# Joining the weighted sums of one attention tile to the scores of the next in a fused attention and MLP kernel, and loading the last batch tile by tile

## The chip, the cores and the metric

The kernel runs on one core of one Trainium2 chip. The metric is the device time of one execution in microseconds (us). The kernel before was run six times: the median is 226.07 us, the lowest 225.56, the highest 226.84. One further number belongs to one of these executions, which took 225.72 us: the hardware profiler recorded it, and everything that is read from a profile below comes from it.

## The reference, cut to what matters

Attention with 4 batches, 8 heads, 768 positions and 64 values a head. A position sees the 128 positions up to itself (the window) and the first four positions of the sequence (the sinks). The heads are laid side by side, and a normalised two-layer MLP with 512 inputs and 2048 hidden values is added to them.

```
scores = q @ k.T / 8
keep   = (pos_k < 4) | (0 <= pos_q - pos_k < 128)
a = softmax(where(keep, scores, -1e9))
x = concat_heads(a @ v)                      # 4 x 768 x 512
xn = (x - mean(x)) / sqrt(var(x) + 1e-6) * g
out = x + relu(xn @ w1) @ w2                 # w1 512x2048, w2 2048x512
```

## The kernel before, in words

The 4 x 768 rows are 24 **tiles** of 128 rows, six to a batch (`RB`); tile t has r = t % 6. The engines are TensorE (PE), VectorE (DVE), ScalarE (ACT) and GpSimd (POOL); SyncE (SP) issues DMAs, and POOL issues the casting loads.

**Attention of a tile** is two TensorE steps with exponentials between them.

- `scores(t)` (lines 548 to 610) multiplies the keys of block r with the queries of blocks r and r + 1, because a key block is seen by its own queries and by those of the next block. A head has 64 values, so the two heads of a pair lie in the two halves of the array's rows: one matmul on rows 0 to 63, one on rows 64 to 127 (L574), with the results in two PSUM banks. Eight matmuls of 256 columns make a tile (128 columns in the last tile of a batch). ACT takes the exponential of each half of four heads (L585, 128x1024), and DVE (L595) or POOL (L597, L600) clears what lies outside the window.
- `values(t)` (lines 620 to 727) sums the values with these weights: 16 matmuls of 65 columns (64 values and a column of ones that gives the divisor), eight with this tile's weights (L641) and eight with those of the tile before (L644). From r = 2 on the sinks lie outside the window, so two more matmuls of 260 columns (L634, one for four heads) add them first; their weights `es` and values `vs` are made once a batch by `sinks`. `es` and `vs` are block structured: heads 0 to 3 fill rows 0 to 63, heads 4 to 7 rows 64 to 127, yet each of the two matmuls runs over all 128 rows. DVE then divides (`recip`, L666 and L668), takes mean and variance (`stat`, L674 and L677) and centres and scales (`cen`, L682). From tile 10 on a DMA transpose on SP's queue (L711) lays the result out for the MLP as `xnt`.

**The MLP** works on groups of 2, 2, 2, 4, 4, 4, 4 and 2 tiles. `up` (L745) makes 128 hidden values for a group of four tiles in four matmuls of 512 columns, and ACT or DVE takes the maximum with zero. `down` (L785) makes a quarter of a tile's output in four matmuls of 512 columns; after the fourth quarter DVE adds x (L798), and SP stores it (L803).

**PSUM** is held by hand. Slots 0 and 2 are the two `wide` tiles of two banks each (kind "pw"); slots 4 to 7 are the four `single` banks (kind "pm"). Scores take both wide tiles (one in the last tile of a batch), `values` takes one wide tile, `up` and `down` take one single bank at a time.

**The order of the work** is a planner's. Every step is an `Op` with a cost for each engine, the steps that it depends on, buffers and a key. `Plan.emit` (lines 57 to 160) goes through a model of the engines, and among the steps that could start first on the engine it takes the one with the lowest key. What it emits is a fixed order for each engine's queue; engines wait by semaphores, in order. `attention(t, key)` (lines 811 to 816) gives the scores of tile t, then `values(t - 1)` as a separate step with nearly the same key, and after the last tile of a batch that tile's own `values`. Batch 0 has an order of its own (lines 849 to 872).

**Loads.** Batches 2 and 3 take q and k in twelve blocks each (`load_qk`, L398, POOL's queue), which DMA transposes on SP's queue turn (`prep`, L481); v comes in six blocks (`load_v`, L407). At most seven loads are under way. The twelve loads of batch 3 stand one behind the other as soon as batch 2 has been turned, and so do its twelve transposes.

Of the kernel before, what the change touches and what calls it, by code (L numbers as in the profile page):

```python
# [8 lines left out]
FP32 = mybir.dt.float32  # L9
# [22 lines left out]
class Plan:  # L32
# [18 lines left out]
    def op(self, engs, fn, deps=(), key=0.0, alloc=(), uses=(), lat=0.0):  # L51
        o = Op(engs, fn, deps, key, alloc, uses)
        o.lat = lat
        self.ops.append(o)
        return o
# [108 lines left out]
def kernel(  # L164
# [28 lines left out]


    GROUPS = [2, 2, 2, 4, 4, 4, 4, 2]
    NB0 = 3
    NG = len(GROUPS)
    FIRST = [sum(GROUPS[:g]) for g in range(NG)]
# [33 lines left out]
    def room_for(buf):  # L232
        return wide[buf.slot // 2] if buf.pool == "pw" else single[buf.slot - 4]
# [252 lines left out]
    def ready(b, hps, klo, khi, qlo, qhi):  # L486

        ends = ((qlo, qhi), (klo, khi))
        if b in CHUNKS:
            w = S // CHUNKS[b]  # L490
            return [prepped[(b, c, hp, x)] for c in range(CHUNKS[b]) for hp in hps for x in range(2)
                    if c * w < ends[x][1] and (c + 1) * w > ends[x][0]]
        return [prepped[(b, r, x)] for x in range(2) for r in range(RB)
                if 128 * r < ends[x][1] and 128 * (r + 1) > ends[x][0]]
# [50 lines left out]

    ebuf = {}

    def scores(t, halves, key):

        b, r = divmod(t, RB)  # L550
        kb = kqb[b]
        last = r == RB - 1
        n = 128 if last else 256

        parts = [halves] if last else [(half,) for half in halves]
        pbs, ebs = [Buf("pw", 0) for _ in parts], [Buf("e", 8) for _ in parts]
        for eb, part in zip(ebs, parts):
            for half in part:
                ebuf[(t, half)] = eb

        added = t < NEG_TILES

        def mm(_):
            for pb, eb, part in zip(pbs, ebs, parts):
                eb.t = epool.tile([128, 2, 512 // n, n], BF16, name="e")
                pb.t = room_for(pb).rearrange("p a (i c) -> p a i c", c=n)
                if added:
                    neg = (neg1 if r else neg0)[:, 0:n].unsqueeze(1).to_broadcast([128, 2, n])
                    for h2 in range(2):
                        nc.tensor.matmul(pb.t[:, h2], lhsT=ident, rhs=neg,  # L570
                                         start=True, stop=False, skip_group_check=True)
                for i, hp in enumerate([2 * half + i for half in part for i in range(2)]):
                    for h2 in range(2):
                        nc.tensor.matmul(pb.t[:, h2, i],  # L574
                                         lhsT=kb.t[64 * h2:64 * (h2 + 1), 1, hp, 128 * r:128 * (r + 1)],
                                         rhs=kb.t[64 * h2:64 * (h2 + 1), 0, hp, 128 * r:128 * r + n],
                                         start=not added, stop=True, skip_group_check=True)

        cost = 0.2 + 0.23 * n / 256 * len(halves) + (0.43 * len(halves) if added else 0.0)
        hps = [2 * half + i for half in halves for i in range(2)]  # L580
        o0 = op({"PE": cost}, mm, ready(b, hps, 128 * r, 128 * (r + 1), 128 * r, 128 * r + n) + [neg_done, edone.get((t - 1, 1)) if last else None], key, pbs + ebs, [kb])

        for pb, eb, part in zip(pbs, ebs, parts):
            def ex(_, pb=pb, eb=eb):
                nc.scalar.activation(eb.t, pb.t, AF.Exp, scale=scale)  # L585

            def first(_, eb=eb):
                ev = eb.t.rearrange("p a i c -> p (a i) c")
                nc.vector.tensor_tensor(ev, ev, mask0.unsqueeze(1).to_broadcast([128, 4, 256]), op=ALU.mult)

            def window(e, eb=eb):
                ev = eb.t.rearrange("p a i c -> p (a i) c")
                m = 1024 // n
                if e == "DVE":
                    nc.vector.tensor_tensor(ev, ev, mask1[:, 0:n].unsqueeze(1).to_broadcast([128, m, n]), op=ALU.mult)  # L595
                    return
                nc.gpsimd.affine_select(out=ev[:, :, 0:128], in_=ev[:, :, 0:128], compare_op=ALU.is_ge,  # L597
                                        fill=0.0, base=0, pattern=[[0, m], [1, 128]], channel_multiplier=-1)
                if n > 128:
                    nc.gpsimd.affine_select(out=ev[:, :, 128:256], in_=ev[:, :, 128:256], compare_op=ALU.is_gt,  # L600
                                            fill=0.0, base=0, pattern=[[0, m], [-1, 128]], channel_multiplier=1)

            o = op({"ACT": 1.02}, ex, [o0], key, (), [eb, pb])
            if not added:
                if r == 0:
                    o = op({"DVE": 0.69}, first, [o, masks_done], key, (), [eb])
                else:
                    o = op({"POOL": 1.28, "DVE": 0.69}, window, [o, masks_done], key, (), [eb])
            for half in part:
                edone[(t, half)] = o  # L610
# [6 lines left out]
    xb, xnb, xtb, mvb, rsb, turned = {}, {}, {}, {}, {}, {}  # L617
    aggr = {}

    def values(t, key):  # L620
        b, r = divmod(t, RB)
        g, ti = where[t]
        vn, vs = vn_buf[b % 2], vs_buf[b % 2]
        pb = Buf("pw", 0)
        xb[t] = Buf("x", 14)
        xnb[t] = Buf("xn", 6)

        def mm(_):
            po = pb.t = room_for(pb)
            pv = po[:, :, 0:4 * (D + 1)].rearrange("p a (h d) -> p a h d", d=D + 1)  # L630
            for half in range(2):
                fresh = True
                if r >= 2:
                    nc.tensor.matmul(po[:, half, 0:4 * (D + 1)], lhsT=esb[b].t[:, 128 * (r - 2):128 * (r - 1)],  # L634
                                     rhs=vs[:, 4 * half:4 * half + 4, :].rearrange("p h d -> p (h d)"),
                                     start=True, stop=False, skip_group_check=True)
                    fresh = False
                for hh in range(4):
                    i, h2 = divmod(hh, 2)
                    h = 4 * half + hh  # L640
                    nc.tensor.matmul(pv[:, half, hh, :], lhsT=weights_of(t, half, i, h2, 0), rhs=vn[:, r, h, 0:D + 1],  # L641
                                     start=fresh and hh == 0, stop=(r == 0), skip_group_check=True)
                    if r > 0:
                        nc.tensor.matmul(pv[:, half, hh, :], lhsT=weights_of(t - 1, half, i, h2, 128),  # L644
                                         rhs=vn[:, r - 1, h, 0:D + 1], start=False, stop=True, skip_group_check=True)

        deps = [edone[(t, half)] for half in range(2)] + [vcast[(b, r)], ones_done]
        uses = [ebuf[(t, half)] for half in range(2)]
# [5 lines left out]
        if r >= 2:  # L654
            deps += [sunk[b], vs_done[b]]
            uses += [esb[b]]
            cost += 0.22
        o = op({"PE": cost}, mm, deps, key, [pb], uses)
        vread[(b, r)] = o

        rc = {}

        def recip(_):
            pv = pb.t[:, :, 0:4 * (D + 1)].rearrange("p a (h d) -> p a h d", d=D + 1)
            rc[0] = small.tile([128, 2, 4], FP32, name="rc")
            nc.vector.reciprocal(rc[0], pv[:, :, :, D])  # L666
            xb[t].t = xpool.tile([128, H, D], BF16, name="xt")
            nc.vector.tensor_tensor(xb[t].t.rearrange("p (a h) d -> p a h d", a=2), pv[:, :, :, 0:D],  # L668
                                    rc[0].unsqueeze(3).to_broadcast([128, 2, 4, D]), op=ALU.mult)

# [11 lines left out]
            nc.vector.scalar_tensor_tensor(xnb[t].t, in0=xf, scalar=mvb[g][:, ti, 0:1], in1=gb,  # L682
                                           op0=ALU.subtract, op1=ALU.mult)

        o = op({"DVE": 0.92}, recip, [o], key, [xb[t]], [pb])
        o = op({"DVE": 0.9}, stat, [o], key, (), [xb[t]])
        aggr[t] = o
        o = op({"DVE": 0.75}, cen, [o, gb_done], key, [xnb[t]], [xb[t]])
# [120 lines left out]


    def attention(t, key):
        scores(t, (0, 1), key)
        if t % RB:
            values(t - 1, key - 0.5)
        if t % RB == RB - 1:
            values(t, key + 1.0)


# [28 lines left out]
    for b in range(B):  # L847
# [25 lines left out]
        if b == 1:  # L873
            for hp in range(HP):
                prep_runs(1, 0, hp, k0 - 12 + 3 * hp)
        else:
            for r in range(RB):
                for x in range(2):
                    load_qk(b, x, r, k0 - 60 + r, [prepped.get((b - 1, RB - 1, 1))])
            for r in range(RB):  # L880
                load_v(b, r, k0 - 50 + r, [prepped[(b, RB - 1, 1)]])
        for r in range(RB):
            attention(RB * b + r, akey(RB * b + r))
            if r == 1:
                sinks(b, akey(RB * b + 2) - 1)
# [54 lines left out]
```

The softmax here doesn't subtract the row's maximum and nothing guards it: scores larger than these inputs give would overflow.

## Time and profile before

| what | value | where from |
|---|---|---|
| median of six runs | 226.07 us | the times |
| profiled execution | 225.72 us | the times |
| its span | 224.0 us | head of the page |
| PE busy | 217.3 us, 97% | part 1 |
| DVE busy, ACT busy, POOL busy | 114.8 us (51%), 111.7 us (50%), 81.2 us (36%) | part 1 |
| granted TensorE clock | full in all slices | part 2 |
| L745 and L785, share of the chain that ended last | 37% and 34% | part 4 |
| L634, L641, L644 (values) busy | 8.7, 15.8, 14.2 us | groups by form |
| L574 (scores) busy | 14.5 us | part 5 |

The span is what the profiler saw from the first to the last instruction; the time has 1.7 us more around it. Matmul records overlap, since a matmul's record reaches to the end of its passage through the array: durations of one matmul (380 ns for 512 columns) are longer than the step from its start to the next start. Steps between starts, in the timeline, are what the engine's time is made of.

### The profile page before, as it was taken

The page shows a single profiled execution, that of the slowest core. Times are in us where ns is not written, and L with a number is a line of the kernel's source. Part 1 is how long each engine was busy: PE and PEld are TensorE (multiplying, and loading weights), DVE is VectorE, ACT ScalarE, POOL GpSimd, SP SyncE. Part 2 cuts the span into 40 slices and gives each one's busy share as a digit, 9 for nine tenths or more (in the row PEclk, how much of TensorE's full clock was granted, in tenths as well). Part 3 has the DMA queues.
Part 4 walks back from the last instruction along what each step waited for, and adds up shares of the span by engine and source line. Part 5 has one row for each costly group of instructions (what it writes and reads, how often), then busy time and mean ns, then how long its engine had stood idle before and what let it go on. Part 6 is the DMA issues. An engine that isn't in the chain of part 4 may idle for free.

```text
span 224.0 us, 4431 instructions
## 1 busy us (share of the span) xinstructions
PE 217.3 (97%) x1805; PEld 122.8 (55%) x1826; DVE 114.8 (51%) x216; ACT 111.7 (50%) x159; POOL 81.2 (36%) x111
## 2 busy tenths in 40 slices
PE   7999999999999999999999999999999999999994
PEld 7465878884546455455544444544454554444852
DVE  5566976054969789589474467470026750021011
ACT  3699775687252576860227762147603156400620
POOL 8985876259420799350823000220006020000000
PEclk9999999999999999999999999999999999999999
DMA  7999999999999799999999111330012130012102
GB/s 172 158 191 197 191 208 204 204 159 155 138 128 258 144 156 132 154 130 182 79 162 233 25 23 48 97 93 0 0 45 77 47 97 0 0 47 94 50 0 94
DMA packets 84774, 25.59 MB, mean 114 GB/s; under 512 B 74385, under 2 KB 81809, under 8 KB 84754
## 3 DMA queue, kind: packets, MB, share of 16 engines
q0 software_dynamic: 59392, 13.24, 66.4%
q1 hardware_dynamic: 24818, 11.67, 26.6%
q10 hardware_dynamic: 544, 0.39, 0.5%
q8 instruction: 14, 0.23, 0.4%
q14 instruction: 6, 0.05, 0.1%
HBM read 27.27 MB, written 6.29 MB: 150 GB/s over the span
## 4 chain that ended last, share of the span: by engine, by line
PE 89%; DVE 6%; DMA 2%; issue 1%; ACT 1%; DVEq 0%
PE single L785 37%; PE single L745 34%; PE wide L574 5%; PE wide L641 2%; PE wide L644 2%; DVE st L674 2%; DVE xt L668 2%; DVE xn L682 2%; DMA xnt<-in_q_dram 2%; PE wide L634 1%; PE wide L457 1%; PE wide L570 1%; PE single L721 1%; PE single L236 1%; PE single L457 1%
## 5 line engine op out<-in xcount | busy, mean ns | idle before, releaser
L745 PE MATMUL single<-xnt,w1s 128*128 128x256 bf16 (+1 forms) x503 | 87.1, 325 | 0.6 <-issue 0.2
L745 PEld LDWEIGHTS <-w1s 128*128 128x128 bf16 x512 | 48.4, 98 | 32.8 <-issue 2.4
L585 ACT ACTIVATE e<-wide 128x1024 bf16<-128x1024 f32 x44 | 43.6, 1022 | 43.3 <-PE wide L574 40.7
L785 PE MATMUL single<-w2s,h1t 128*128 128x512 bf16 x249 | 57.6, 379 | 0.4
L798 DVE SCALAR_TENSOR_TENSOR ot<-single,rs,xt 128x512 f32<-128x512 f32 (+2 forms) x25 | 18.2, 729 | 61.6 <-PE single L785 45.1
L754 ACT ACTIVATE h1t<-single 128x512 bf16<-128x512 f32 x60 | 35.8, 597 | 21.1 <-PE single L745 21.1
L785 PEld LDWEIGHTS <-h1t 128*128 128x128 bf16 x256 | 24.0, 98 | 28.2 <-issue 1.1
L785 PE MATMUL single<-w2s,h1n 128*128 128x512 bf16 (+2 forms) x139 | 29.6, 355 | 0.3
L754 ACT ACTIVATE h1n<-single 128x512 bf16<-128x512 f32 x30 | 17.9, 597 | 22.2 <-PE single L745 22.0
L597 POOL TENSOR_SCALAR_AFFINE_SELECT e<-e 128x512 bf16<-128x512 bf16 (+1 forms) x10 | 7.0, 697 | 45.0 <-ACT e L585 45.0
L407 POOL DMA_DIRECT2D vn<-in_v_dram x24 | 21.7, 922 | 2.0 <-DMA qkn<-in_q_dram 1.0
L694 POOL TENSOR_SCALAR ve<-mv 128x2 f32<-128x2 f32 (+1 forms) x8 | 4.6, 574 | 46.5 <-DVE mv L677 46.3
L595 DVE TENSOR_TENSOR e<-e,mask 128x1024 bf16<-128x1024 bf16 x22 | 15.9, 722 | 8.7 <-ACT e L585 8.5
L785 PEld LDWEIGHTS <-h1n 128*128 128x128 bf16 x144 | 12.6, 98 | 12.3 <-issue 1.3
L682 DVE SCALAR_TENSOR_TENSOR xn<-xt,mv,gb 128x512 bf16<-128x512 bf16 x24 | 18.3, 768 | 0.7
L674 DVE BATCH_NORM_STATS2 st<-xt 128x6 f32<-128x512 bf16 x24 | 16.7, 695 | 0.8
L668 DVE TENSOR_TENSOR xt<-wide,rc 128x512 bf16<-128x512 f32 x24 | 16.6, 691 | 0.8
L641 PE MATMUL wide<-vn,e 128*128 128x65 bf16 x192 | 15.8, 193 | 0.0
L641 PEld LDWEIGHTS <-e 128*128 128x128 bf16 x192 | 13.7, 97 | 2.6 <-issue 0.2
L574 PE MATMUL wide<-qkt 64*128 64x256 bf16 (+1 forms) x192 | 14.5, 263 | 0.0
L644 PE MATMUL wide<-vn,e 128*128 128x65 bf16 x160 | 14.2, 193 | 0.0
L398 POOL DMA_DIRECT2D qkn<-in_q_dram x12 | 11.3, 938 | 3.6 <-DMA qkn<-in_k_dram 3.1
(66 smaller groups left out, 161.1 us busy)
## 6 DMA issues: line engine op xcount, KB each, us to landing
out_dram<-ot SPq DMA_DIRECT2D x23, 256.0 KB, 2.2
vn<-in_v_dram POOLq DMA_DIRECT2D x24, 128.0 KB, 8.0
w1s<-in_moe_w_ch_dram POOLq DMA_DIRECT2D x4, 512.0 KB, 11.2
w2s<-in_moe_w_ch_dram POOLq DMA_DIRECT2D x4, 512.0 KB, 15.0
qkn<-in_q_dram POOLq DMA_DIRECT2D x12, 128.0 KB, 7.5
qkn<-in_k_dram POOLq DMA_DIRECT2D x12, 128.0 KB, 7.1
qkn<-in_q_dram POOLq DMA_DIRECT2D x1, 768.0 KB, 16.2
qkn<-in_k_dram POOLq DMA_DIRECT2D x1, 768.0 KB, 19.3
```

The costliest lines, as they stand in the source:

```text
L407: nc.gpsimd.dma_start(vn_buf[b % 2][:, r, :, 0:D], v[b, :, 128 * r:128 * (r + 1), :].rearrange("h p d -> p h d"))
L574: nc.tensor.matmul(pb.t[:, h2, i], lhsT=kb.t[64 * h2:64 * (h2 + 1), 1, hp, 128 * r:128 * (r + 1)], rhs=kb.t[64 * h2:64 * (h2 + 1), 0, hp, ...
L585: nc.scalar.activation(eb.t, pb.t, AF.Exp, scale=scale)
L641: nc.tensor.matmul(pv[:, half, hh, :], lhsT=weights_of(t, half, i, h2, 0), rhs=vn[:, r, h, 0:D + 1], start=fresh and hh == 0, stop=(r == 0 ...
L644: nc.tensor.matmul(pv[:, half, hh, :], lhsT=weights_of(t - 1, half, i, h2, 128), rhs=vn[:, r - 1, h, 0:D + 1], start=False, stop=True, ski ...
L668: nc.vector.tensor_tensor(xb[t].t.rearrange("p (a h) d -> p a h d", a=2), pv[:, :, :, 0:D], rc[0].unsqueeze(3).to_broadcast([128, 2, 4, D] ...
L674: nc.vector.bn_stats(st, xf)
L682: nc.vector.scalar_tensor_tensor(xnb[t].t, in0=xf, scalar=mvb[g][:, ti, 0:1], in1=gb, op0=ALU.subtract, op1=ALU.mult)
L745: nc.tensor.matmul(pb.t[:, n * i:n * (i + 1)], lhsT=w1s[:, j, 128 * (h0 + i):128 * (h0 + i + 1)], rhs=xtb[g].t[:, j, 0:n], start=(j == 0), ...
L754: nc.scalar.activation(hb.t, pb.t, AF.Relu)
L785: nc.tensor.matmul(pb.t[:, 0:n], lhsT=hidden(g, ht, ti), rhs=w2s[:, ht, c0:c1], start=(ht == 0), stop=(ht == NH1 - 1))
L798: nc.vector.scalar_tensor_tensor(ob.t[:, 0:n], in0=pb.t[:, 0:n], scalar=rsb[g][:, ti:ti + 1], in1=xb[t].t.rearrange("p h d -> p (h d)")[:, ...
```

## The change

`values(t - 1)` is no longer a step of its own where it can be joined: `values(..., joined=True)` returns a `Lead` that `scores(t)` runs first, in one planner step, with the dependencies, buffers and costs of both. This holds for t = 11 to 23, so the joined sums are those of tiles 10 to 22; the last tile of batch 1 and of batch 2 is now joined to the first scores of the next batch. Tiles 6 to 9 (`ALONE`), batch 0 and tile 23 keep separate steps.

A joined sum lies in two single banks and not in one wide tile, and DVE divides it in two halves with two instructions each. Its sink matmuls come behind the others and run on 64 rows each, half 0 on rows 0 to 63 and half 1 on rows 64 to 127, with an accumulator bank each.

The q, k and v blocks of batch 3 are asked for one at a time, each with the key of a tile of batch 2 and, from the second on, behind the masks of the tile before (`seen`).

```diff
+    ALONE = (6, 7, 8, 9)
...
-    def scores(t, halves, key):
+    def scores(t, halves, key, lead=None):
...
         def mm(_):
+            if lead:
+                lead.fn(None)
...
+        if lead:
+            o0 = op({"PE": cost + lead.cost}, mm, deps + lead.deps, key, lead.alloc + pbs + ebs, [kb] + lead.uses)
+            lead.rest(o0)
+        else:
+            o0 = op({"PE": cost}, mm, deps, key, pbs + ebs, [kb])
...
-    def values(t, key):
+    def values(t, key, joined=False):
...
-        pb = Buf("pw", 0)
+        banks = [Buf("pm", 0), Buf("pm", 0)] if joined else [Buf("pw", 0)]
...
+        def sink(half, fresh):
+            rows = slice(64 * half, 64 * (half + 1)) if joined else slice(0, 128)
+            nc.tensor.matmul(sums[half], lhsT=esb[b].t[rows, 128 * (r - 2):128 * (r - 1)],
+                             rhs=vs[rows, 4 * half:4 * half + 4, :].rearrange("p h d -> p (h d)"),
+                             start=fresh, stop=not fresh, skip_group_check=True)
...
             for half in range(2):
                 fresh = True
-                if r >= 2:
+                if r >= 2 and not joined:
+                    sink(half, True)
                     fresh = False
...
+            if r >= 2 and joined:
+                for half in range(2):
+                    sink(half, False)
...
-            cost += 0.22
-        o = op({"PE": cost}, mm, deps, key, [pb], uses)
+            cost += 0.12 if joined else 0.22
+        if joined:
+            lead = Lead()
+            lead.fn, lead.deps, lead.alloc, lead.uses, lead.cost = mm, deps, banks, uses, cost
+            lead.rest = lambda o: normalise(t, key, o, banks, sums)
+            return lead
+        normalise(t, key, op({"PE": cost}, mm, deps, key, banks, uses), banks, sums)
...
+            if len(banks) == 2:
+                for half in range(2):
+                    pv = sums[half].rearrange("p (h d) -> p h d", d=D + 1)
+                    rc[half] = small.tile([128, 4], FP32, name=f"rc{half}")
+                    nc.vector.reciprocal(rc[half], pv[:, :, D])
+                    nc.vector.tensor_tensor(xb[t].t[:, 4 * half:4 * half + 4], pv[:, :, 0:D],
+                                            rc[half].unsqueeze(2).to_broadcast([128, 4, D]), op=ALU.mult)
+                return
...
-        o = op({"DVE": 0.92}, recip, [o], key, [xb[t]], [pb])
+        o = op({"DVE": 0.92 if len(banks) == 1 else 1.22}, recip, [o], key, [xb[t]], banks)
...
     def attention(t, key):
-        scores(t, (0, 1), key)
-        if t % RB:
+        alone = t - 1 in ALONE
+        scores(t, (0, 1), key, None if alone or t == RB else values(t - 1, key, True))
+        if alone:
             values(t - 1, key - 0.5)
-        if t % RB == RB - 1:
+        if t == NT - 1:
             values(t, key + 1.0)
...
-            for r in range(RB):
+            for r in range(RB if b == 2 else 0):
                 for x in range(2):
-                    load_qk(b, x, r, k0 - 60 + r, [prepped.get((b - 1, RB - 1, 1))])
+                    load_qk(b, x, r, k0 - 60 + r)
-            for r in range(RB):
+            for r in range(RB if b == 2 else 0):
                 load_v(b, r, k0 - 50 + r, [prepped[(b, RB - 1, 1)]])
         for r in range(RB):
+            if b == B - 2:
+                t = RB * (b + 1) + r
+                seen = [edone[(RB * b + r - 1, 0)]] if r else []
+                for x in range(2):
+                    load_qk(b + 1, x, r, akey(t) - 45, seen + [prepped[(b, RB - 1, 1)]])
+                load_v(b + 1, r, akey(t) - 40, seen)
             attention(RB * b + r, akey(RB * b + r))
```

More of the change, by code (lines that the diff above doesn't have):

```diff
@@ L580, in scores @@
         hps = [2 * half + i for half in halves for i in range(2)]
-        o0 = op({"PE": cost}, mm, ready(b, hps, 128 * r, 128 * (r + 1), 128 * r, 128 * r + n) + [neg_done, edone.get((t - 1, 1)) if last else None], key, pbs + ebs, [kb])
+        deps = ready(b, hps, 128 * r, 128 * (r + 1), 128 * r, 128 * r + n) + [neg_done, edone.get((t - 1, 1)) if last else None]
+        if lead:
[3 more added lines that the diff above has]
+            o0 = op({"PE": cost}, mm, deps, key, pbs + ebs, [kb])
         for pb, eb, part in zip(pbs, ebs, parts):
@@ L618 @@
     aggr = {}
-    def values(t, key):
+    class Lead:
+        pass
+    def values(t, key, joined=False):
         b, r = divmod(t, RB)
@@ L623, in values @@
         vn, vs = vn_buf[b % 2], vs_buf[b % 2]
-        pb = Buf("pw", 0)
+        banks = [Buf("pm", 0), Buf("pm", 0)] if joined else [Buf("pw", 0)]
+        sums = []
         xb[t] = Buf("x", 14)
         xnb[t] = Buf("xn", 6)
+        def sink(half, fresh):
[3 more added lines that the diff above has]
+                             start=fresh, stop=not fresh, skip_group_check=True)
         def mm(_):
-            po = pb.t = room_for(pb)
-            pv = po[:, :, 0:4 * (D + 1)].rearrange("p a (h d) -> p a h d", d=D + 1)
+            po = [room_for(i) for i in banks]
+            po = po if joined else [po[0][:, i] for i in range(2)]
+            sums[:] = [i[:, 0:4 * (D + 1)] for i in po]
             for half in range(2):
                 fresh = True
-                if r >= 2:
-                    nc.tensor.matmul(po[:, half, 0:4 * (D + 1)], lhsT=esb[b].t[:, 128 * (r - 2):128 * (r - 1)],
-                                     rhs=vs[:, 4 * half:4 * half + 4, :].rearrange("p h d -> p (h d)"),
-                                     start=True, stop=False, skip_group_check=True)
+                if r >= 2 and not joined:
+                    sink(half, True)
                     fresh = False
+                pv = sums[half].rearrange("p (h d) -> p h d", d=D + 1)
                 for hh in range(4):
@@ L640, in mm @@
                     h = 4 * half + hh
-                    nc.tensor.matmul(pv[:, half, hh, :], lhsT=weights_of(t, half, i, h2, 0), rhs=vn[:, r, h, 0:D + 1],
+                    nc.tensor.matmul(pv[:, hh, :], lhsT=weights_of(t, half, i, h2, 0), rhs=vn[:, r, h, 0:D + 1],
                                      start=fresh and hh == 0, stop=(r == 0), skip_group_check=True)
                     if r > 0:
-                        nc.tensor.matmul(pv[:, half, hh, :], lhsT=weights_of(t - 1, half, i, h2, 128),
-                                         rhs=vn[:, r - 1, h, 0:D + 1], start=False, stop=True, skip_group_check=True)
+                        nc.tensor.matmul(pv[:, hh, :], lhsT=weights_of(t - 1, half, i, h2, 128),
+                                         rhs=vn[:, r - 1, h, 0:D + 1], start=False, stop=not (joined and r >= 2),
+                                         skip_group_check=True)
+            if r >= 2 and joined:
+                for half in range(2):
+                    sink(half, False)
         deps = [edone[(t, half)] for half in range(2)] + [vcast[(b, r)], ones_done]
@@ L656, in values, with normalise @@
             uses += [esb[b]]
-            cost += 0.22
-        o = op({"PE": cost}, mm, deps, key, [pb], uses)
+            cost += 0.12 if joined else 0.22
[5 more added lines that the diff above has]
+        normalise(t, key, op({"PE": cost}, mm, deps, key, banks, uses), banks, sums)
+    def normalise(t, key, o, banks, sums):
+        b, r = divmod(t, RB)
+        g, ti = where[t]
         vread[(b, r)] = o
@@ L663, in recip @@
         def recip(_):
-            pv = pb.t[:, :, 0:4 * (D + 1)].rearrange("p a (h d) -> p a h d", d=D + 1)
+            xb[t].t = xpool.tile([128, H, D], BF16, name="xt")
+            if len(banks) == 2:
+                for half in range(2):
+                    pv = sums[half].rearrange("p (h d) -> p h d", d=D + 1)
+                    rc[half] = small.tile([128, 4], FP32, name=f"rc{half}")
[3 more added lines that the diff above has]
+                return
+            pv = room_for(banks[0])[:, :, 0:4 * (D + 1)].rearrange("p a (h d) -> p a h d", d=D + 1)
             rc[0] = small.tile([128, 2, 4], FP32, name="rc")
             nc.vector.reciprocal(rc[0], pv[:, :, :, D])
-            xb[t].t = xpool.tile([128, H, D], BF16, name="xt")
             nc.vector.tensor_tensor(xb[t].t.rearrange("p (a h) d -> p a h d", a=2), pv[:, :, :, 0:D],
```

## The prediction

> **What bounds the kernel now.** I read the page's head, parts 1 and 4 first, then the busy time by stretches.
>
> ```profile
> span 224.0 us, 4431 instructions
> PE 217.3 (97%) x1805; PEld 122.8 (55%) x1826; DVE 114.8 (51%) x216; ACT 111.7 (50%) x159; POOL 81.2 (36%) x111
> PE 89%; DVE 6%; DMA 2%; issue 1%; ACT 1%; DVEq 0%
> ```
>
> ```profile
> 90.00:130.00 40.00, 39.71 (x292) 19.29 (x297) 25.62 (x48) 20.97 (x31) 12.78 (x16) 1.00 1.34 134
> 130.00:170.00 40.00, 39.74 (x248) 18.87 (x250) 16.55 (x29) 17.07 (x25) 3.19 (x5) 1.00 0.14 44
> ```
>
> The second fence has the stretch, its length, and the busy time of PE, weight loads, DVE, ACT and POOL. PE leaves 0.3 us of 40 empty, at full clock; the others are half idle. So only work taken off PE, or a gap on PE, moves the time. Busy records overlap, so I went to the timeline of PE for the steps from start to start.
>
> ```profile
> 59.85 2.54 PE L785 MATMUL single<-w2s,h1n 128*128 128x512 bf16 x11
> 62.32 0.61 PE L574 MATMUL wide<-qkt 64*128 64x256 bf16 x8
> 62.86 1.04 PE L785 MATMUL single<-w2s,h1n 128*128 128x512 bf16 x4
> 63.74 0.39 PE L721 MATMUL single<-ident,xn 128*128 128x128 bf16 x4
> ```
>
> A 512-column matmul steps on by 0.216 us (the chain has 3.45 us for 16). Eleven from 59.85 would let the next start at 62.22; the scores start at 62.32, so going from 128-row matmuls to 64-row ones costs 0.10. Eight matmuls of 256 columns then take 0.54, coming back included. One after the other, at the 0.11 that a 260-column one takes below, they would need 0.87: the two row halves run side by side, a pair for the price of one. Four pairs are 0.43, so coming back costs about 0.11.
>
> ```profile
> 68.06 0.27 PE L634 MATMUL wide<-vs,es 128*128 128x260 bf16 x1
> 68.17 0.19 PE L641 MATMUL wide<-vn,e 128*128 128x65 bf16 x1
> ...
> 68.42 0.27 PE L634 MATMUL wide<-vs,es 128*128 128x260 bf16 x1
> 68.53 0.19 PE L641 MATMUL wide<-vn,e 128*128 128x65 bf16 x1
> ...
> 68.78 1.02 PE L785 MATMUL single<-w2s,h1n 128*128 128x512 bf16 x4
> ```
>
> A `values` of a tile with sinks takes 0.72 (68.06 to 68.78), of which the two sink matmuls are 0.11 each.
>
> ```profile
> 23.01 0.19 PE L644 MATMUL wide<-vn,e 128*128 128x65 bf16 x1
> 23.13 0.39 PE L574 MATMUL wide<-qkt 64*128 64x256 bf16 x4
> ```
>
> Here scores follow `values` directly: 0.12 from start to start where two 65-column matmuls stand 0.03 apart. Entering costs 0.09, the same as behind the MLP.
>
> **Part by part, on PE.** *Joining.* Apart, a tile costs 0.72 + (0.10 + 0.54 + 0.01) = 1.37, with one entry into the 64-row form and one return. Joined, it has the same one entry and one return: 16 sums 0.50, entry 0.10, a sink pair, scores 0.54 + 0.01. Joining alone saves nothing on PE.
>
> *Row-tiled sinks.* Two matmuls of 260 columns, 0.22, become one pair in two PSUM banks, the layout of the L574 pairs: 0.11 saved a tile. They stand between the sums and the scores, so they need no entry of their own. Of the 13 joined tiles (10 to 22), those with r >= 2 are 10, 11, 14 to 17 and 20 to 22: nine. 9 x 0.11 = **0.99 us**. Bounds: nothing saved if the pair does not overlap; no reason for more than 0.99. I take the pair of L574, the same form 4 columns shorter. The Trainium skill's page "TensorE: Matmul & The Clock Gate" (Measured speedup vs the span model) speaks against a full factor: four row tiles gave 3.07, not 4. With that share of the ideal two would give 1.5, and the nine tiles an estimated 0.7 us. The L574 rows, 0.54 for eight, do not show such a loss.
>
> *Loads.* In the timeline of SP the twelve transposes of batch 3 stand ahead of three `xnt` transposes (tiles 11 to 13):
>
> ```profile
> 87.03 18.50 SPq L481 DMA_TRANSPOSE qkt<-qkn  x12
> 105.62 5.20 SPq L711 DMA_TRANSPOSE xnt<-xn  x3
> ```
>
> The last of the three is issued at 109.6 and lands 5.5 us later (the tile view of `xnt`), at 115.1; the first `up` of that group waits for it:
>
> ```profile
> 113.95 1.24 PE L785 MATMUL single<-w2s,h1t 128*128 128x512 bf16 x5
> 115.22 1.02 PE L745 MATMUL single<-xnt,w1s 128*128 128x512 bf16 x3
> ```
>
> Five steps from 113.95 end at 115.03: PE lost 0.19. In the changed kernel's SP order two or three batch-3 transposes stand between neighbouring `xnt` ones. Tile 13's `xnt` stands behind block r = 2, whose load waits for a mask of tile 13's scores. I put these scores near 89 us, its mask near 92, landing near 100 (median 7.3), the transposes near 103, `xnt` landed by 109, and the `up` at 114.5: **0.19 us** saved, with 5 us to spare. If the loads were that much later, 0.19 would come back and more.
>
> *What is late next.* On PE nothing else above 0.03 us stood out after 50 us in before (steps of 0.43 where 0.216 is due are missing records). New waits can come from three places.
>
> (a) The joined block waits for the masks of tile t - 1, and the scores of t are queued behind it on PE. Where blocks follow most closely, the changed order has five `down` steps between them: 5 x 0.865 + 1.26 = 5.6 us from block to block. The scores start 0.70 after the block (0.50 + 0.10 + 0.10), ACT 0.43 later (168.91 to 169.34 in the trace), the two exponentials take 2 x 1.02, and the last mask is due at 3.2. On DVE (0.72) it is ready at 3.9. On POOL (0.65 + 0.69) at 4.5, but for tiles 15 and 16 the order puts a load (0.94) that waits for the first mask (2.95) ahead of it: 5.3 to 5.7 with the slowest L600 (1.07). So two blocks sit within 0.2 us of a wait. Bounds 0 and 0.4 for the two; I take **0.1**.
>
> (b) Banks: the block takes two of the four single banks. DVE frees them with 2 x (0.20 + 0.42) = 1.25 us, where one division took 0.92 (0.42 is the 128x260 multiply of L526, the nearest row). The 13 x 0.33 = 4 us more of DVE lie beside PE, as DVE is idle for 109 us; what counts is the third MLP step behind a block, which in several places reuses one of the two banks. In the order this is 1.7 us of MLP plus 0.6 of scores behind the sums: enough if DVE starts within about 1.1 us, and the division mostly stands first or behind one instruction. I count 0; the price if that cover goes is in a rival.
>
> (c) Group 6's first `up` comes closer behind tile 21: six `down` steps and a block, 6.1 us, between the issue of its transpose and its use, where before had 8.5. Landing took 2.4 in this stretch. Nothing.
>
> The seven more transposes ahead of stores on SP hold back one store at a time, and there are three `ot` buffers: nothing. The tail is the same.
>
> **Sum.** 225.72 (profiled execution) - 0.99 - 0.19 + 0.1 = 224.64. The median is 0.35 above that execution: **225.0 us**, 0.5% less. About 0.3%, 0.68 us, can be told from no change.
>
> **Rivals.** *The masks are late* (0.17): (a) is larger. POOL clears 13 masks where it cleared 10, and one L600 took 1.07 beside a DVE mask of 1.00, where the means are 0.69 and 0.72. If four blocks wait 0.25 each, 1.0 of 1.18 is gone: 225.9, no change. For it: DVE and POOL orders are filled with loads just there. Against: before had the same masks in front of `values` and PE did not wait once for them.
>
> *The sink pair does not overlap* (0.05), so that the change does not do what it says: only 0.19 remains, 225.9. Against: all L574 pairs overlap.
>
> *Banks decide* (0.10, slower). If DVE reaches the division behind another tile's mean, centring and mask (0.69 + 0.18 + 0.75 + 0.72 = 2.3 us), the third step behind a block waits about 1.2 us at a bank. It turns the gain into a loss from 0.14 us a block (1.18 + 0.68 over 13 blocks) if all blocks wait, or from 0.5 in the four that stand among `up` steps, where ACT also has two exponentials between the maxima. With 0.8 in those four: 225.0 + 3.2 = 228.2. The Trainium skill's page "TensorEngine Tiling (Array Packing)" (PSUM Bottleneck) warns of this: tiling speeds up TensorE, not the emptying of PSUM. Against it: L798 shows DVE idle 59 us just before it, much of it next to such blocks.
>
> **How the numbers follow.** Forecast 0.68 (faster); late masks 0.17 and no overlap 0.05 (both about no change); banks 0.10 (slower). Faster 0.68, within 0.3% 0.22, slower 0.10. The range takes in the full gain with no wait and a lucky 0.4 below, 224.5, and both cases of no change with their spread, 226.3; the bank case is left out.
>
> **What would show it.** In the changed profile: the sink line with 64x260 matmuls, 18 of them, about 0.11 us from the first of a pair to the scores behind it; scores 0.12 behind the last 65-column matmul where no sink stands; the first `up` of group 4 one step behind the last `down`; PE's lost time after 50 us under 0.2 us. I would be wrong if PE sits in front of the block's first sum (masks), in front of an L745 or L785 matmul behind a block (banks), or if the two sinks of a pair start 0.11 apart.

## The result, and the profile after

The changed kernel takes **224.9 us** (median of 21 runs, 224.51 to 225.53), the kernel before 226.35 us (47 runs, 225.51 to 227.25). The ratio is 0.994, 95% interval 0.9929 to 0.995: 1.1 to 1.6 us faster. A second comparison gave 0.9945 (0.9921 to 0.9968). Ratios and intervals, here and below, leave out runs more than 1.5% above the fastest of their kernel. The profiled execution took 225.46 us, its span is 223.8 us. The head and parts 1 and 4 of its page:

```profile
span 223.8 us, 4479 instructions
PE 216.9 (97%) x1805; PEld 124.6 (56%) x1826; DVE 114.7 (51%) x239; ACT 112.2 (50%) x159; POOL 84.8 (38%) x116
PE 90%; DVE 7%; issue 2%; ACT 0%; DVEq 0%
```

The kernel is bound as before: `down` (L827) has 37% of the chain that ended last and `up` (L787) 34%. In the kernel before the 37% are those of `down` (L785) and the 34% those of `up` (L745); the table above has the two the other way round. The spans differ by 0.2 us only, though the medians differ by more: this execution took longer to reach the MLP. The first `down` matmul starts at 52.33 us here and at 51.42 in the profile before, and up to there the instructions of the two kernels are the same. So I compare **from the start of the first `down` matmul to the start of the last one** in the timeline of PE: 169.17 us before (51.42 to 220.59), 167.98 after (52.33 to 220.31). That is 1.19 us less. The second profile of the changed kernel gives 167.98 again, with its first `down` at 52.46. I use this measure, the *stretch*, for all runs below.

A joined block in the timeline of PE of the kernel after, tile 15's sums and tile 16's scores:

```profile
107.92 0.19 PE L661 MATMUL single<-vn,e 128*128 128x65 bf16 x1
...
108.37 0.20 PE L664 MATMUL single<-vn,e 128*128 128x65 bf16 x1
108.50 0.28 PE L644 MATMUL single<-vs,es 64*128 64x260 bf16 x2
108.62 0.60 PE L577 MATMUL wide<-qkt 64*128 64x256 bf16 x8
109.15 0.39 PE L827 MATMUL single<-w2s,h1t 128*128 128x512 bf16 x1
```

The last sum and the first sink matmul stand 0.13 apart where sums stand 0.03 apart: the way into the 64-row form, 0.10. From the pair to the scores it is 0.12, for both sink matmuls. All nine pairs look like this one: their two matmuls start 3 to 4 ns apart, and the scores 0.12 behind the first of them. The block takes 1.23 to the next `down`, and 0.01 more in the step behind that.

The first `up` of group 4:

```profile
114.73 0.81 PE L827 MATMUL single<-w2s,h1t 128*128 128x512 bf16 x3 [0.16 <-issue]
115.38 5.34 PE L787 MATMUL single<-xnt,w1s 128*128 128x512 bf16 x24
```

Three steps of 0.216 from 114.73 end at 115.38: the 0.19 us that PE lost here is gone.

### The profile page after: what moved, and what is told of

It reads as the page before. It is cut to its first block, busy times and chain, and to the rows that moved or that the text cites. A ratio compares the mean times of both kernels' runs of the same rounds, so it can differ in the third digit from the quotient of the medians.

```text
span 223.8 us, 4479 instructions
## 1 busy us (share of the span) xinstructions
PE 216.9 (97%) x1805; PEld 124.6 (56%) x1826; DVE 114.7 (51%) x239; ACT 112.2 (50%) x159; POOL 84.8 (38%) x116
## 4 chain that ended last, share of the span: by engine, by line
PE 90%; DVE 7%; issue 2%; ACT 0%; DVEq 0%
PE single L827 37%; PE single L787 34%; PE wide L577 5%; PE single L237 3%; DVE st L716 2%; DVE xt L710 2%; DVE xn L724 2%; PE single L661 1%; PE single L664 1%; PE wide L458 1%; PE wide L573 1%; PE single L763 1%; PE single L458 1%; PE wide L661 1%; PE single L644 1%
## 5 line engine op out<-in xcount | busy, mean ns | idle before, releaser
L787 PE MATMUL single<-xnt,w1s 128*128 128x256 bf16 (+1 forms) x505 | 86.7, 325 | 0.4
L787 PEld LDWEIGHTS <-w1s 128*128 128x128 bf16 x512 | 48.7, 98 | 33.6 <-issue 1.9
L827 PE MATMUL single<-w2s,h1t 128*128 128x512 bf16 x247 | 55.8, 379 | 0.9 <-issue 0.8
L827 PEld LDWEIGHTS <-h1t 128*128 128x128 bf16 x256 | 24.3, 98 | 29.8 <-issue 1.5
L605 POOL TENSOR_SCALAR_AFFINE_SELECT e<-e 128x512 bf16<-128x512 bf16 (+1 forms) x13 | 9.2, 711 | 60.6 <-ACT e L593 60.6
L827 PE MATMUL single<-w2s,h1n 128*128 128x512 bf16 (+2 forms) x139 | 29.4, 355 | 0.3
L827 PEld LDWEIGHTS <-h1n 128*128 128x128 bf16 x144 | 12.7, 98 | 12.3 <-issue 1.1
L724 DVE SCALAR_TENSOR_TENSOR xn<-xt,mv,gb 128x512 bf16<-128x512 bf16 x24 | 18.8, 783 | 0.7
L603 DVE TENSOR_TENSOR e<-e,mask 128x1024 bf16<-128x1024 bf16 x19 | 13.1, 690 | 6.5 <-ACT e L593 6.5
L661 PEld LDWEIGHTS <-e 128*128 128x128 bf16 x192 | 13.2, 98 | 2.5
L703 DVE RECIPROCAL rc<-single 128x4 f32<-128x4 f32 x26 | 4.6, 177 | 16.9 <-PE single L644 10.6
L664 PEld LDWEIGHTS <-e 128*128 128x128 bf16 x160 | 10.7, 97 | 1.7
L399 POOL DMA_DIRECT2D qkn<-in_k_dram x12 | 10.8, 903 | 1.8 <-DMA w2s<-in_moe_w_ch_dram 1.7
```

What stands on the lines that cost most here:

```text
L399: nc.gpsimd.dma_start(dst[:, r], (q, k)[x][b, :, 128 * r:128 * (r + 1), :].rearrange("h p d -> p h d"))
L661: nc.tensor.matmul(pv[:, hh, :], lhsT=weights_of(t, half, i, h2, 0), rhs=vn[:, r, h, 0:D + 1], start=fresh and hh == 0, stop=(r == 0), ski ...
L787: nc.tensor.matmul(pb.t[:, n * i:n * (i + 1)], lhsT=w1s[:, j, 128 * (h0 + i):128 * (h0 + i + 1)], rhs=xtb[g].t[:, j, 0:n], start=(j == 0), ...
L827: nc.tensor.matmul(pb.t[:, 0:n], lhsT=hidden(g, ht, ti), rhs=w2s[:, ht, c0:c1], start=(ht == 0), stop=(ht == NH1 - 1))
```

## The experiments

The theory: the gain is nine row-tiled pairs at 0.11 us and one wait of 0.19 us, and joining serves to give the pairs an entry into the 64-row form that the scores pay for anyway. The rivals: the joining itself saves; the loads are the larger part; banks or masks decide.

### Joined, with sinks over all rows

```diff
-            rows = slice(64 * half, 64 * (half + 1)) if joined else slice(0, 128)
+            rows = slice(0, 128)
```

> The changed kernel in the same order of instructions, but each of the two sink matmuls of a joined block runs over all 128 rows, so the two follow one another. Theory (the gain is the row-tiled pair): nine blocks are 0.11 us longer each, the time is 1.0 us above the changed kernel, 0.2 us under the kernel before (ratio to before 0.999). In the timeline 0.22 us lie between the first sink and the drain ahead of the scores. Rival (the joining itself saves, and the form of the sinks is worth little): the ratio stays near 0.994 to 0.996.

Ratio 0.9984 (0.9963 to 1.0005), stretch 169.00: 1.02 above the changed kernel, 0.17 under before. The timeline of its first joined block:

```profile
79.00 0.20 PE L664 MATMUL single<-vn,e 128*128 128x65 bf16 x1
79.03 0.38 PE L644 MATMUL single<-vs,es 128*128 128x260 bf16 x2
79.35 0.40 PE L577 MATMUL wide<-qkt 64*128 64x128 bf16 x8
```

From the first sink to the scores are 0.32 us: twice 0.11 and the entry of 0.10. In the changed kernel the entry and the pair are 0.22 together. The joining without the row tiling saves only the wait: loads_alone, below, has the same stretch (168.98) without any joining.

### Row-tiled sinks without joining

In the kernel before, for tiles from 10 on, instead of the two in front of the sums:

```diff
...
+            if r >= 2 and t >= 10:
+                for half in range(2):
+                    rows = slice(64 * half, 64 * (half + 1))
+                    nc.tensor.matmul(po[:, half, 0:4 * (D + 1)], lhsT=esb[b].t[rows, 128 * (r - 2):128 * (r - 1)],
+                                     rhs=vs[rows, 4 * half:4 * half + 4, :].rearrange("p h d -> p (h d)"),
+                                     start=False, stop=True, skip_group_check=True)
...
```

> The kernel before in its order of instructions, values and scores apart, but for tiles 10 to 23 the two sink matmuls are a row-tiled pair behind the sums. Theory (a pair saves 0.11 us but needs its own way into the 64-row form and back, 0.10 and 0.11): ten tiles, of which one (tile 10) already stands ahead of scores, so nine times about 0.10 us more and once 0.11 less, 0.8 us above the kernel before (ratio 1.0035). Rival (the pair alone is what saves, joining is not needed): about 1.1 us under the kernel before (ratio 0.995).

Ratio 1.0028 (0.9999 to 1.0056), stretch 170.66, 1.48 above before. Timeline of PE:

```profile
85.30 0.19 PE L644 MATMUL wide<-vn,e 128*128 128x65 bf16 x1
85.42 0.29 PE L650 MATMUL wide<-vs,es 64*128 64x260 bf16 x2
85.64 0.39 PE L752 MATMUL single<-xnt,w1s 128*128 128x512 bf16 x1
```

0.13 into the pair and 0.22 out of it, where two sinks over all rows would take 0.22 in all and need neither: 0.10 lost a tile in nine tiles, less 0.11 in tile 10, whose pair already stands ahead of scores: about 0.8. The other 0.7 is the wait before group 4's first `up`, 0.87 in this execution where it was 0.19 before; why it grew is not shown. The rival, that the pair alone saves, falls. The Trainium skill's page "TensorEngine Tiling (Array Packing)" (Key Properties) says that changing the tiling mode drains TensorE. The trace agrees in that each way costs 0.10, about what a pair saves.

### The loads alone, and the joining with the old loads

The first has only the load part of the diff on the kernel before, the second has all but that part.

> The kernel before with the second part of the change alone: the blocks of batch 3 are loaded one by one. Theory: the wait of 0.19 us of the first up of group 4 for tile 13's transposed result goes, nothing else: 0.2 us under before (ratio 0.999), within what can be told from no change; the timeline shows no lost time at that place. Rival (the loads are the larger part of the gain): ratio 0.996 or less.

Ratio 0.9993 (0.9971 to 1.0015), stretch 168.98, 0.19 under before, and no lost time at group 4: six `down` steps of 0.216 from 114.74 end at 116.04, and the first `up` starts at 116.03. Its stretch and that of joined_full_sinks differ by 0.02: the joining itself is worth nothing that can be seen.

> The changed kernel with the loads of batch 3 as before, twelve transposes in a row on SP. Theory: the nine pairs keep their 0.99 us, and a wait of 0.2 us or somewhat more before the first up of group 4 comes back, so a ratio of 0.995 to 0.996. Rival (the joined order needs the spread loads, since SP holds back transposed results for longer than PE has other work): PE waits 1 us or more for transposed results and the ratio is 1.0 or above.

Here the rival held. Twelve runs lie between 225.9 and 231.4 us, median 229.0, 1.2% above the median before; the ratio of 1.0025 (0.9987 to 1.0063) is that of the six lowest. In the profiled execution (228.6 us) the stretch is 171.64, 3.66 above the changed kernel, and one wait in the timeline of PE is all of it:

```profile
114.25 0.81 PE L827 MATMUL single<-w2s,h1t 128*128 128x512 bf16 x3 [0.16 <-issue]
118.56 0.81 PE L787 MATMUL single<-xnt,w1s 128*128 128x512 bf16 x3 [3.50 <-DMA xnt<-xn]
```

Tile 13's transpose was issued at 109.2, earlier than in the kernel before (109.6), but it landed 9.2 us after its issue, not 5.5. What differed was POOL: it had the six v blocks of batch 3 just ahead of the transposes of tiles 12 and 13, from 105.39 on, where the kernel before had them from 108.26 on, behind tile 12's.

### When the v blocks come

> The kernel of joined_old_loads with one more dependency: the six v blocks of batch 3 wait for the masks of tile 16, so that POOL issues them near 110 us and not at 105. Theory (the 3.7 us that PE waited there come from the v blocks, which reach the DMA rings just ahead of the transposes of tiles 12 and 13, so that these landed 8 to 9 us after their issue where the kernel before had 5.2 to 5.5): landing falls to about 5.5 and the wait before the first up of group 4 to 0.5 us or less; ratio to before 0.995 to 0.998. Rival (the twelve transposes in a row on SP are enough for the wait, in the joined order): the transposes still land near 118 us and PE waits 3 us or more.

This run told nothing apart. On every engine and queue its instructions come in the order of joined_old_loads, so it is that kernel once more, in an execution that reached the first `down` 0.51 us later (52.36 after 51.85); the v blocks "moved" by these 0.5 us. The wait stayed: 2.5 us, the two transposes landing after 7.6 and 8.4 us (ratio 1.0109, 1.006 to 1.0158; six runs from 227.0 to 231.9 us). The stretch of 172.15 is 4.17 above the changed kernel; 1.7 of that lies behind the wait: the granted TensorE clock was half from 118.5 to 121.9 us, and eight steps of `up` took 0.43 where 0.216 is due. In joined_old_loads the wait was longer and the clock stayed full.

The added dependency on tile 16's masks is one of the planner's only. It can set the order in POOL's queue, and here did not; on the chip the loads did not wait for the mask. Timelines of POOL and DVE in this run, the v blocks and tile 16's first mask:

```profile
105.89 5.36 POOL L408 DMA_DIRECT2D vn<-in_v_dram  x6
```

```profile
109.33 0.69 DVE L603 TENSOR_TENSOR e<-e,mask 128x1024 bf16<-128x1024 bf16 x1 [0.15 <-ACT e L593]
```

So the next one asks for the blocks so late that one more mask stands ahead of them in POOL's queue:

```diff
-                load_v(b, r, k0 - 50 + r, [prepped[(b, RB - 1, 1)]])
+                load_v(b, r, k0 - 50 + r, [prepped[(b, RB - 1, 1)]] + ([turned[13]] if b == 3 else []))
```

> As joined_old_loads, but the six v blocks of batch 3 wait until tile 13's transposed result has landed (in joined_old_loads_v_later they moved by 0.5 us only, so that run could not tell the two theories apart). Theory (v blocks on the DMA rings make the transposes of tiles 12 and 13 land late): these now land 5 to 6 us after their issue, PE waits 0.5 us or less before the first up of group 4, and a wait of up to 1 us may come before the sums of tile 18, whose v block now comes late. Rival (the row of twelve transposes is enough): the transposes are issued near 109 us as before and still land near 118, PE waits 2.5 us or more.

Ratio 0.995 (0.9928 to 0.9971), stretch 167.98, the changed kernel's, with the twelve transposes still in a row. (This run was on another chip than joined_old_loads; each ratio is to the kernel before on the same chip.) POOL's timeline in joined_old_loads, and there the tile view of `xnt` for the two transposes issued between 107.5 and 110.5:

```profile
105.39 5.37 POOL L408 DMA_DIRECT2D vn<-in_v_dram  x6
```

```profile
DMA to landing us min/median/max: 7.8/8.5/9.2
```

The same two views of joined_old_loads_v_last, with the mask (two instructions) that POOL now has first:

```profile
110.11 0.64 POOL L605 TENSOR_SCALAR_AFFINE_SELECT e<-e 128x512 bf16<-128x512 bf16 x1 [4.33 <-ACT e L593]
110.70 0.64 POOL L608 TENSOR_SCALAR_AFFINE_SELECT e<-e 128x512 bf16<-128x512 bf16 x1
111.28 5.37 POOL L408 DMA_DIRECT2D vn<-in_v_dram  x6
```

```profile
DMA to landing us min/median/max: 3.5/3.9/4.4
```

With the v blocks behind them the same two transposes, in the same order on SP, land 3.4 us (tile 12) and 5.7 us (tile 13) sooner after their issue, and the wait is gone. So it was the v blocks ahead of the transposes, together with the row that had put the transposes there. By what way the loads hold the transposes back is not shown.

> The changed kernel with the q and k blocks of batch 3 one by one, as changed, but its six v blocks in a row as before. Theory (tile 13's transposed result must only not stand behind twelve transposes on SP): no wait before the first up of group 4, ratio 0.994 to 0.995 as the changed kernel. Rival (v blocks in a row hurt wherever they fall): a wait of 1 us or more for a transposed result, ratio 0.998 or more.

Ratio 0.9959 (0.994 to 0.9977), stretch 168.44. No wait at group 4, as the theory has it; 0.45 us are lost elsewhere, since v blocks in a row at the end come late for tile 18's sums:

```profile
130.44 0.42 PE L661 MATMUL single<-vn,e 128*128 128x65 bf16 x8 [0.29 <-DMA vn<-in_v_dram]
```

### Banks: the division three times and twice

```diff
-                    nc.vector.tensor_tensor(xb[t].t[:, 4 * half:4 * half + 4], pv[:, :, 0:D],
-                                            rc[half].unsqueeze(2).to_broadcast([128, 4, D]), op=ALU.mult)
+                    for _ in range(3):
+                        nc.vector.tensor_tensor(xb[t].t[:, 4 * half:4 * half + 4], pv[:, :, 0:D],
+                                                rc[half].unsqueeze(2).to_broadcast([128, 4, D]), op=ALU.mult)
```

> The changed kernel in the same order, but DVE's division of each half of a joined tile is done three times over, with the same result: the two banks come free about 0.8 and 1.7 us later, and DVE has 13 x 1.7 = 22 us more. Theory (DVE lies beside PE, and the banks come free with 0.4 us or more to spare): some blocks now wait, 0.3 to 1 us each where the third MLP step behind a block takes one of its banks or where the mask of the last tile stands behind the division; 2 to 8 us in all, and PE's waits stand in front of L787 and L827 matmuls (banks) or of a block's first sum (masks). Rival (there is much more cover than that): under 1 us more than the changed kernel, ratio 0.995 to 0.998.

Ratio 1.0187 (1.0165 to 1.0209), stretch 173.28: 5.3 us lost. The waits view of PE between 52 and 220 us (total, times, longest):

```profile
PE single L788 <- DVE xt L705: 2.1, 4, 1.1
...
PE single L828 <- DVE xt L705: 0.7, 1, 0.7
PE wide L661 <- DVE e L603: 0.7, 1, 0.7
PE single L534 <- DVE ks L507: 0.6, 1, 0.6
```

`up` and `down` wait for the division to free a bank, the last tile's sums for a mask behind it, and the sinks' scores of batch 2 for their keys, which DVE makes. None of these rows is in the changed kernel. From start to start, `up` and `down` lost 3.8 us of the 5.3, the mask cost 0.85 and the sinks' scores 0.68.

> The changed kernel in the same order, DVE's division of each half of a joined tile done twice: the banks come free about 0.4 and 0.85 us later. In slow_division (0.8 and 1.7 us) PE lost 4.6 us, nearly all of it in front of up and down matmuls that waited for the division. Theory (cover of about half a microsecond at the blocks among up steps): of the waits of slow_division those of 0.5 us and less go, the larger ones shrink by about 0.85: 0.3 to 1 us lost in all, ratio 0.996 to 0.999. Rival (the waits come from DVE's total of work and not from single banks): about half of slow_division's loss, 2.3 us or more, ratio above 1.003.

Ratio 0.9961 (0.9941 to 0.9981), stretch 168.28: 0.30 lost, in one step of an `up` (0.52 where 0.216 is due, at 82.06). This `up` takes the second bank of tile 10's block, which came free 0.9 us later than in the changed kernel; so the cover at the tightest bank is about 0.6 us. The loss sits at single places: twice the delay costs not twice but 18 times as much.

### All tiles joined

`ALONE = ()`.

> The changed kernel with no tile left alone in batches 1 to 3: tiles 6 to 9 are joined too. Theory (every joined tile with r >= 2 saves 0.11 us as long as PE does not wait): tiles 8 and 9 add 0.22 us, 1.0 us under the changed kernel's own gain of 1.2 makes 1.4 us under before, ratio 0.993 to 0.994. Rival (there, where up and down of two-tile groups and PE transposes also use single banks, two banks fewer make PE wait): the gain of 0.22 is lost and PE loses 0.3 us or more at a bank or a mask between 50 and 80 us; ratio 0.995 or above.

Ratio 0.9945 (0.9929 to 0.9962), 224.74 us, stretch 167.86. No wait between 50 and 80 us. The stretch is 0.12 shorter than the changed kernel's, not 0.22; where the other 0.10 went is not shown. By the time it can't be told from the changed kernel. It is faster than before, and no better version than the changed kernel is shown.

### The changed kernel again

> The changed kernel once more, for a second profile: from the first down matmul to the last one the kernel before took 169.17 us and the changed one 167.98. Theory (the gain is nine pairs and one wait, and the start varies by up to 1 us from execution to execution): 167.9 to 168.1 again, whatever the span is; ratio 0.993 to 0.996.

Ratio 0.9945 (0.9921 to 0.9968), stretch 167.98: as expected.

## Why the prediction was right

It forecast 225.0 us, 1.07 less than the median before; 224.9 was measured. The stretch shortened by 1.19 = 9 x 0.11 + 0.19, which is its sum without the 0.1 for new waits. That the time itself came within 0.1 us is in part luck: the six runs that it started from had a median of 226.07, the 47 later ones 226.35, so by the medians the gain is 1.45, not 1.07. The stretch is the firmer figure.

- **Row-tiled sinks, 0.99 us: right.** The pair costs one matmul's step. Taking the row tiling away adds 1.02, 0.11 a tile over the nine. The estimate of 0.7 us by the 3.07 for four tiles of the Trainium skill's page "TensorE: Matmul & The Clock Gate" (Measured speedup vs the span model) is not what the trace shows: there the measurement decides.
- **Joining saves nothing on PE itself: right,** and joined_full_sinks beside loads_alone shows it (169.00 and 168.98). That the pair needs the joining is shown by apart_row_sinks.
- **Loads, 0.19 us: right as the difference to before,** shown by loads_alone. In the changed kernel tile 13's transpose was issued at 103.18 and landed at 107.78, 7.6 us ahead of its `up`. What it did not price is what the load part does inside the joined order. It asked what late loads would cost, and not what the old loads would: there they cost 3.7 us in the profiled execution, and the whole gain. The joined order needs the v blocks out of the way of these transposes; the load part does that, and so do the old loads with late v blocks.
- **(a) masks, 0.1 us: the one term that was mis-sized; it measured 0.** The step that failed is the load "that waits for the first mask" ahead of the POOL masks of tiles 15 and 16. POOL's timeline of the kernel after:

```profile
102.31 0.97 POOL L399 DMA_DIRECT2D qkn<-in_q_dram  x1
105.56 0.63 POOL L605 TENSOR_SCALAR_AFFINE_SELECT e<-e 128x512 bf16<-128x512 bf16 x1 [2.28 <-ACT e L593]
106.16 0.63 POOL L608 TENSOR_SCALAR_AFFINE_SELECT e<-e 128x512 bf16<-128x512 bf16 x1
...
108.50 0.90 POOL L399 DMA_DIRECT2D qkn<-in_q_dram  x1
111.12 0.63 POOL L605 TENSOR_SCALAR_AFFINE_SELECT e<-e 128x512 bf16<-128x512 bf16 x1 [1.72 <-ACT e L593]
111.70 0.63 POOL L608 TENSOR_SCALAR_AFFINE_SELECT e<-e 128x512 bf16<-128x512 bf16 x1
```

  The loads ahead of the masks went at 102.31 and 108.50 without waiting for the tile's first mask; POOL then stood idle until ACT's exponential was there. `seen` is a dependency of the planner, and the blocks behind (107.92 and 113.48) had the mask 1.13 and 1.15 us before them, not 0.2.
- **(b) banks, counted 0: right, with less cover than it named.** The division measured 2 x (0.18 + 0.43) = 1.2 us (L703 and L704), and no bank made PE wait. It gave DVE about 1.1 us to begin; at the tightest bank about 0.6 us were to spare (double_division). Its rival put 1.2 us on a division that begins 2.3 us late. With the division three times over, the longest loss from start to start was 1.2 us too (the idle time in the waits view is 1.1), but there the bank came about 1.8 us late, with 0.6 us of cover: that the two agree is in part chance.

## What to carry to other kernels

Where TensorE leaves no gap, count steps from start to start and put half-height matmuls next to others of their form: a pair saves one step (0.11 us here), and going into that form and back costs about two (0.10 each way). When steps are merged in a planned order, look at what each DMA queue has ahead of the results that the bound engine waits for next; a load order that was free in the old order can cost more than the merge gains. A dependency that only a planner sees can order a queue, and makes nothing wait on the chip.

## What the runs showed that I had not expected

Six v blocks on POOL's queue just ahead of two DMA transposes on SP's queue made these land after 7.6 to 9.2 us (two profiles), and behind them after 3.5 to 4.4 (one). And the start of this kernel varies: up to the first `down` the same instructions took 51.42 to 52.46 us in the profiles of before and after, nearly as much as the change gains.
